# An attention, expert and MLP kernel: weight loads moved to the head of a step, three kinds of loads one or two steps later

## The chip, the cores and the metric

The program runs on one core of a Trainium2 chip. What counts is the device time of one execution, in microseconds (us). Beside the times there is one execution with a profile; its times are counted from the start of its span. Engines are called as the profile calls them: PE (TensorE), PEld (its weight loads), DVE (VectorE), ACT (ScalarE), POOL (GpSimd), SP (SyncE, which issues nearly all loads).

## What is computed

```python
def _attn_ref(q, k, v, f):                       # B, H, S, D = 2, 8, 576, 64
    scores = q @ k.T / sqrt(D)
    cum = np.cumsum(np.log(np.clip(f, 0.0001, 1.0)), axis=-1)
    scores = np.where(causal, -1e9, scores + cum[:, :, :, None] - cum[:, :, None, :])
    attn = exp(scores - max); attn = attn / (sum + 1e-9)
    return attn @ v
def _moe_ref(x, domain_probs, w1, w2):           # N, D, E, F = 1152, 512, 4, 1024
    p = domain_probs / (domain_probs.sum(-1) + 1e-9)
    for e in range(E): out += p[:, e:e+1] * (np.maximum(x @ w1[e], 0) @ w2[e])
def _moe2_ref(x, w_in, w_out):                   # d_ff = 2048
    h = x @ w_in
    return (h / (1 + exp(-1.702 * h))) @ w_out
```

The three follow each other: attention, four experts weighted per token, and an MLP. The code above is shortened from the reference.

## The kernel before

**Precision.** Operands are split into two parts, a rounded high one and a low rest (hi and lo), and a product takes three matmuls: hi by hi, lo by hi, hi by lo. Rounding a weight is an ACT instruction (`whi`, line 71), the low part a subtraction on DVE (`wlo`, line 249). Queries are rounded on POOL (`qhi`, line 68) and their low parts are made there (`qlo`, line 596); keys are rounded on ACT, their low parts made half on DVE and half on POOL (`ks`, line 578).

**Stages.** The tokens stand in four chunks. Chunk 0 (256 tokens) has its attention first. Then `attention()` works off the rest as a sequence of units: of chunk 1 three units for each pair of heads (384, 512 and 576 keys wide; 12 units, counted from 0 here), then of the second batch five units for each pair (20 units). A step of this generator emits scores for unit i (PE, line 652), the maximum on DVE (line 682, which also adds the gate row `cb` or, in the units of 576, `cbs`), the exponential of unit i - 1 on ACT (line 698) and its normalisation on POOL (line 708), the transposes of unit i - 2 (PE, line 726, copied out of PSUM by ACT, `ph`), and the product with the values of unit i - 3 (PE, line 756, tile `x`, rounded into `xh` and `xl`).

Into these steps the first layers (`emit_l1`, PE line 934) and second layers (`emit_l2`, line 1099) of the experts are mixed for chunks whose attention is done: the main loop walks the list `seq` of such visits and steps, and `pull()` takes as many attention steps as are due. So PE has the expert matmuls as filling for its waits in the attention. From about 200 us on only experts and the MLP are left; there some products are computed jointly for two chunks with sums and differences of weights (`emit_joint`, line 974, combined on DVE in `u` and `jc`), and the MLP's weights, which come as 64-bit numbers, are converted in steps of one instruction (`mlp_convert`, lines 418 to 433, tiles `cvt`, `wf`, `cvd`). How many of these steps are emitted behind a step of the main loop is counted in `cv_due`.

**What sets the order.** The engines take their instructions in the order that a scheduler gives them from the order of emission and its own model; only some parts are pinned by hand. SP's queue is in order too: a load that waits for its buffer holds up those behind it. Loads of weights go in pairs of 512 KB into four buffers (`wst`): when both halves of a pair are split, `rest()` puts the function `load_pair` on the list `pair_due`, and before the change it was called from the next `rest()` or from `split_next`.

**Loads of the attention.** In a step i, for the pair of heads whose first unit is i + 3, keys and queries are prepared (`prep_parts`, `prep_queries`), and the keys and queries (`kq`, `qr`) of the pair after it are loaded (`load_heads`) at the end of the step. For the pair that begins at i + 2 `load_cum` loads two `cb` tiles (128x512) and the `cbs` tile (128x576, in two halves). For the pair that begins at i the values (`vd`) are loaded.

Of the kernel before, what the change touches and what calls it, by code (L numbers as in the profile page):

```python
# [15 lines left out]
B, H, S, D = 2, 8, 576, 64  # L16
# [34 lines left out]
def attn_moe_mlp(ctx: ExitStack, tc: tile.TileContext, qk0, qk1, qk2, v0, vp, fg, dp, wa_moe, wb_moe, wa_mlp, wb_mlp, out):  # L51
# [36 lines left out]
    late = {}  # L88
# [506 lines left out]
            r, h, l = (t.rearrange("p (t g k) -> p t g k", g=2, k=128)[64 * g:64 * g + 64, :, g] for t in (raw, f(hi), lo))  # L595
            nc.gpsimd.tensor_sub(l, r, h)

    def load_cum(p, h0):

        cs, b, s0 = p  # L600
        st = pairs[p, h0]
        r = b * H + h0
        st["cb"] = [cb_p.tile([128, 512], F32, tag="cb", name="cb") for _ in range(2)]
        for g, cb in enumerate(st["cb"]):
            load(cb, cumd[r + g:r + g + 1, :512].to_broadcast([128, 512]))
        st["cbs"] = cbs_p.tile([128, S], F32, tag="cbs", name="cbs")
        for g in range(2):
            load(st["cbs"][64 * g:64 * g + 64], cumd[r + g:r + g + 1, :].to_broadcast([64, S]))
# [203 lines left out]
    def first_step(i):  # L812

        n = len(first_seq)
        p, h0 = passes[1], 0
        prep = [(7, lambda: prep_keys(p, h0, 0)), (7, lambda: prep_keys(p, h0, 1)), (9, lambda: prep_keys(p, h0, 2)),
                (9, lambda: prep_queries(p, h0, 1, (0,))), (9, lambda: prep_queries(p, h0, 1, (1,)))]
        for j in (0, 1) if i == 0 else (i + 1,):
            if j < n:
                emit_scores(*first_seq[j])  # L820
        if 3 <= i < n + 3:
            emit_pv(0, i - 3)
        if i >= 7 and x_used[0] < x_made[0] and x_used[0] < 3:
            emit_first(x_used[0])
            x_used[0] += 1
        if i < n:
            emit_max(*first_seq[i])
            emit_exp(*first_seq[i])
        if 1 <= i <= n:
            emit_norm(*first_seq[i - 1])  # L830
        if 2 <= i < n + 2:
            first_copy(i - 2)
        if 3 <= i < n + 3:
            emit_x2(0, i - 3)
        split_rest()
        for kind, p0 in (("a", 2), ("b", 6)):
            if 0 <= i - p0 < 4:
                split_w(kind, 0, i - p0)
                pass
        for j, fn in prep:  # L840
            if i == j:
                fn()
        if i < len(FILL):
            turn(FILL[i])
        if 1 <= i <= n:
            first_tr(i - 1)
        if i == 0:
            load_cum(p, h0)
        if i == 8:
            load_heads(passes[1], 2)  # L850
        if i == 9:
            load_values(p, h0)

    def attention():
# [9 lines left out]
        for i, (c, u) in enumerate(seq):  # L864
            if True:
                first_q.setdefault((pass_of[c], u[0][0], c), i)
        nxt = list(first)
        per_unit = dict(scores=emit_scores, max=emit_max, exp=emit_exp, norm=emit_norm, tr=emit_tr)
        by_last = dict(pv=emit_pv, x2=emit_x2)
        names = sorted(STAGES, key=lambda k: -STAGES[k])  # L870
        for i in range(len(seq) + L_X2 + 1):
# [8 lines left out]
                    prep_queries(*k)  # L880
            for k in [k for k in nxt if first[k] == i + 2]:
                load_cum(*k)
            for k in [k for k in nxt if first[k] == i and i]:
                load_values(*k)
            for k in names:
                j = i - STAGES[k]
                if k in per_unit:
# [9 lines left out]
            for k in new:  # L897
                n = nxt.index(k) + 1
                if n < len(nxt):
                    load_heads(*nxt[n])  # L900
            yield done


# [447 lines left out]
    cv_due = [0]  # L1351
    in_turn(emit_first, 3, True)
    for i, (kind, v_, b, c) in enumerate(seq):
# [22 lines left out]
            j_gen = emit_joint(v_, b, m, ts_rest, 0, 1) if kind == 7 else emit_joint(v_, b, m, ts, *visits[v_][1][:2])  # L1376
        n_steps = steps(kind, v_, b, c)
        for g in range(n_steps):
            if kind in (2, 6):
                split_until("b", v_, range(4))  # L1380
            elif kind not in (4, 5):
# [55 lines left out]
            if late:  # L1437

                if sums_at.get(u, 0) < 2:
# [4 lines left out]
                    else:  # L1444
                        rate = (0.75 if kind == 4 else 0) if v_ < v_all else 1.4 if v_ == v_all else 1.75
                    if kind == 3 and v_ in both_joint and c == EXP[0]:
                        cv_due[0] += g in (0, 2)
                    cv_due[0] += rate * (4 / n_steps) if rate != 11 / 4 else 3 * (g < 3)
                while cv_due[0] >= 1:
                    in_turn(next, cv_gen[0], None)  # L1450
# [66 lines left out]
```

## Time and profile before

| | |
|---|---|
| median of 3 runs | 692.91 us (691.76 to 693.12) |
| the profiled execution | 691.82 us, span 690.1 us |
| PE busy | 681.2 us, 99% of the span, 3937 matmuls |
| PEld, DVE, ACT, POOL busy | 600.0, 531.4, 354.3, 239.4 us |
| granted clock of PE | 0.999 of full speed |
| chain of work that ended last | PE 92%, DVE 4%, the rest 1% or less each |

The profiled execution's own time is 1.7 us more than its span. Matmuls are pipelined and their ends are modelled: a PE that is busy all the time may still lose some time between matmuls, and differences between starts tell more than the busy times.

### The profile page before, as it was taken

Reading aid. Unit: us, or ns where it says so; the run is one execution under the profiler, and the core shown is the slowest. Engines: PE = TensorE matmul, PEld = TensorE weight load, DVE = VectorE, ACT = ScalarE, POOL = GpSimd, SP = SyncE. Lnnn points to the kernel's source line nnn. Section 1 sums busy time; section 2 is a strip of 40 time slices with the busy share of each in tenths; the row PEclk is TensorE's granted clock in tenths of the full one; section 3 lists DMA queues with packets and bytes.
Section 4 is the critical chain, followed back from the end, with each engine's and each line's share of the span. In section 5 each row is a group of like instructions: output and inputs, shape, how many; then the busy total and the mean of one; then the engine's idle time right before and its main releaser. Section 6 shows DMA issues by size and latency. Waiting matters only on the chain.

```text
span 690.1 us, 11086 instructions
## 1 busy us (share of the span) xinstructions
PE 681.2 (99%) x3937; PEld 600.0 (87%) x3937; DVE 531.4 (77%) x1097; ACT 354.3 (51%) x821; POOL 239.4 (35%) x286
## 2 busy tenths in 40 slices
PE   8999999999999999999999999999999999999997
PEld 4797888888888998998889898898899998998986
DVE  6896777777789688676887878767799989998632
ACT  5778767667543645635246254362456454452420
POOL 6887576532233454543035324133003300120000
PEclk9999999999999999999999999999999999999999
DMA  8697726313542244144631422403332544441012
GB/s 251 229 301 249 258 93 238 99 61 93 168 138 61 51 134 129 48 128 157 196 107 47 144 86 82 146 33 107 123 107 77 153 138 136 154 153 61 1 47 91
DMA packets 41063, 87.59 MB, mean 127 GB/s; under 512 B 3720, under 2 KB 5776, under 8 KB 40752
## 3 DMA queue, kind: packets, MB, share of 16 engines
q1 hardware_dynamic: 40680, 84.75, 38.2%
q0 software_dynamic: 288, 2.10, 0.8%
q8 instruction: 31, 0.51, 0.3%
q14 instruction: 24, 0.20, 0.1%
q10 hardware_dynamic: 40, 0.04, 0.0%
HBM read 73.98 MB, written 12.88 MB: 126 GB/s over the span
## 4 chain that ended last, share of the span: by engine, by line
PE 92%; DVE 4%; POOL 1%; ACT 1%; DMA 1%; issue 1%; SPq 0%; POOLq 0%; DVEq 0%
PE m L1099 41%; PE m L974 23%; PE m L934 15%; PE s L652 4%; PE x L756 4%; PE t L726 3%; PE m L1255 1%; DMA dpraw<-in_dp_dram 1%; DVE acc L1143 0%; POOL ks L578 0%; DVE hl L1088 0%; DVE cvd L431 0%; DVE wlo L249 0%; PE m L951 0%; DVE wf L433 0%
## 5 line engine op out<-in xcount | busy, mean ns | idle before, releaser
L1099 PE MATMUL m<-whi,hh 128*128 128x512 f32 x392 | 109.6, 392 | 0.0
L1099 PE MATMUL m<-wlo,hh 128*128 128x512 f32 x392 | 108.0, 391 | 0.0
L1099 PE MATMUL m<-whi,hl 128*128 128x512 f32 x392 | 107.2, 390 | 0.0
L249 DVE TENSOR_TENSOR wlo<-wst,whi 128x512 fp32r<-128x512 f32 x132 | 100.3, 774 | 5.1 <-ACT whi L71 4.6
L985 POOL TENSOR_TENSOR hl<-jc,hh 128x320 fp32r<-128x320 f32 (+1 forms) x60 | 53.1, 888 | 141.1 <-ACT hh L71 141.1
L71 ACT ACTIVATE whi<-wst 128x512 fp32r<-128x512 f32 x136 | 80.7, 625 | 23.7 <-PE m L1099 13.5
L1099 PEld LDWEIGHTS m<-wlo,hh 128*128 128x128 f32 x392 | 73.4, 188 | 15.5
L1099 PEld LDWEIGHTS m<-whi,hl 128*128 128x128 f32 x392 | 73.5, 188 | 15.5
L1099 PEld LDWEIGHTS m<-whi,hh 128*128 128x128 f32 x392 | 71.9, 188 | 12.4
L270 POOL TENSOR_TENSOR sr<-wst 128x256 f32<-128x256 f32 x20 | 17.9, 893 | 156.2 <-DMA wst<-wm 58.0
L708 POOL TENSOR_SCALAR e<-e,sm 128x128 f32<-128x128 f32 (+4 forms) x72 | 46.7, 660 | 60.3 <-DVE sm L706 35.9
L983 ACT ACTIVATE jc<-jc 128x320 f32<-128x320 f32 (+1 forms) x60 | 27.1, 451 | 54.8 <-DVE jc L980 54.3
L1143 DVE SCALAR_TENSOR_TENSOR acc<-m,dpn,acc 128x512 f32<-128x512 f32 x63 | 46.5, 744 | 9.0 <-PE m L1099 8.9
L934 PE MATMUL m<-xh,whi 128*128 128x256 f32 (+2 forms) x256 | 51.7, 316 | 0.0
L934 PE MATMUL m<-xl,whi 128*128 128x256 f32 (+2 forms) x256 | 51.7, 316 | 0.0
L934 PE MATMUL m<-xh,wlo 128*128 128x256 f32 (+2 forms) x256 | 51.0, 313 | 0.0
L698 ACT ACTIVATE e<-e,mx 128x128 f32<-128x128 f32 (+4 forms) x72 | 41.7, 581 | 11.6 <-DVE mx L682 11.1
L934 PEld LDWEIGHTS m<-xh,whi 128*128 128x128 f32 x256 | 41.6, 189 | 1.4
L934 PEld LDWEIGHTS m<-xl,whi 128*128 128x128 f32 x256 | 41.5, 189 | 0.8
L1082 ACT ACTIVATE m<-m 128x384 f32<-128x384 f32 x48 | 23.0, 480 | 37.3 <-DVE m L980 35.6
L934 PEld LDWEIGHTS m<-xh,wlo 128*128 128x128 f32 x256 | 41.5, 189 | 0.7
L71 ACT ACTIVATE ph<-t 128x256 f32<-128x256 f32 (+4 forms) x81 | 28.9, 405 | 17.6 <-PE t L726 17.2
(173 smaller groups left out, 1502.5 us busy)
## 6 DMA issues: line engine op xcount, KB each, us to landing
wst<-in_wa_moe_dram SPq DMA_DIRECT2D x28, 512.0 KB, 3.8
wst<-in_wb_moe_dram SPq DMA_DIRECT2D x28, 512.0 KB, 4.5
mst<-in_wa_mlp_dram SPq DMA_DIRECT2D x16, 512.0 KB, 3.7
wm<-wf SPq DMA_DIRECT2D x32, 256.0 KB, 3.9
mst<-in_wb_mlp_dram SPq DMA_DIRECT2D x16, 512.0 KB, 4.1
wst<-wm SPq DMA_DIRECT2D x16, 512.0 KB, 3.9
cb<-cumd SPq DMA_DIRECT2D x16, 256.0 KB, 4.0
qr<-in_qk_dram SPq DMA_DIRECT2D x8, 384.0 KB, 5.1
```

The lines of the kernel that those rows point to most:

```text
L71: return nc.scalar.activation(out=out, in_=in_, func=AF.Copy)
L249: (nc.gpsimd if v_ == 0 and kind == 'a' and g < 4 else nc.vector).tensor_sub(lf, raw, f(hf))
L652: nc.tensor.matmul(pt[:, :z - a], lhsT=lr[i][0], rhs=lr[i][1], start=i == 0 and not (both and pt is not bank), stop=i == n - 1, skip_group ...
L698: nc.scalar.activation(out=e[:, off:off + w], in_=e[:, off:off + w], func=AF.Exp, scale=-1.0, bias=mx, accum_out=sm[:, 0, k:k + 1])
L708: nc.gpsimd.tensor_scalar(out=e[:, off:off + w], in0=e[:, off:off + w], scalar1=sm[:, 0, i:i + 1], scalar2=1.0, op0=ALU.mult, op1=ALU.mult)
L756: nc.tensor.matmul(pt[64 * g:64 * g + 64, o:n], lhsT=lhsT, rhs=rhs, start=i == 0, stop=i == nk - 1)
L934: nc.tensor.matmul(p[:, :n], lhsT=w[:, k, :], rhs=x[c][:, k, :], start=(j == 0 and k == 0), stop=(j == 2 and k == 3))
L974: nc.tensor.matmul(p[:, :WN], lhsT=w[a][:, k, :], rhs=x[z][:, k, :], start=start and j == 0 and k == 0, stop=stop and j == 2 and k == 1, s ...
L983: nc.scalar.activation(out=r, in_=r, func=AF.Relu)
L985: nc.gpsimd.tensor_sub(hl[:, g, :], r, f(hh[:, g, :]))
L1099: nc.tensor.matmul(p, lhsT=h_tile(v_, b, c, j, x, k), rhs=wb[v_, k][w].rearrange("p a c -> p (a c)"), start=i == 0 and k == 0, stop=i == 2 ...
L1143: nc.vector.scalar_tensor_tensor(out=a, in0=p, scalar=d, in1=a, op0=ALU.mult, op1=ALU.add)
```

## The change

Four things are changed; the work that is computed stays the same, and so does the number of instructions on each engine.

1. In the main loop, until the attention is done, a `load_pair` that is owed is called at the head of each step, ahead of the attention steps that are pulled there.
2. `load_heads` for the next pair goes on a list `owed` and is called one attention step later, behind `load_cum` and ahead of `load_values`.
3. `load_cum` loads only the two `cb` tiles; the `cbs` tile is loaded by the new `load_last`, called with `load_values`, two steps later. For the first pair it stays where it was.
4. In the first step of the joint halves of expert visits (`both_joint`, first chunk) one conversion step is emitted behind g = 0 and g = 2; in the first of these visits now behind g = 0 only.

```diff
-    def load_cum(p, h0):
+    def load_cum(p, h0, first=False):
...
         for g, cb in enumerate(st["cb"]):
             load(cb, cumd[r + g:r + g + 1, :512].to_broadcast([128, 512]))
+        if first:
+            load_last(p, h0)
+
+    def load_last(p, h0):
...
         st["cbs"] = cbs_p.tile([128, S], F32, tag="cbs", name="cbs")
         for g in range(2):
             load(st["cbs"][64 * g:64 * g + 64], cumd[r + g:r + g + 1, :].to_broadcast([64, S]))
...
             for k in [k for k in nxt if first[k] == i + 2]:
                 load_cum(*k)
+            for k in owed:
+                load_heads(*k)
+            owed.clear()
             for k in [k for k in nxt if first[k] == i and i]:
                 load_values(*k)
+                load_last(*k)
...
                 if n < len(nxt):
-                    load_heads(*nxt[n])
+                    owed.append(nxt[n])
...
         for g in range(n_steps):
+            if not late:
+                while pair_due:
+                    pair_due.pop()()
...
                     if kind == 3 and v_ in both_joint and c == EXP[0]:
-                        cv_due[0] += g in (0, 2)
+                        cv_due[0] += g in (0, 2)[:1 + (v_ > v_all + 1)]
```

**What it moves in the attention, on SP and POOL.** SP's queue before, from the keys of the fourth pair of chunk 1; the second `kq` with the `qr` of 512 and of 768 belongs to the first pair of the second batch, and the `cb x2` behind it is the one that stands at 52.30 us in the trace:

```order
L77 DMA kq<-in_qk_dram 128x576
L77 DMA qr<-in_qk_dram 128x768
L77 DMA cb<-cumd 128x512 x2
L77 DMA cbs<-cumd 64x576 x2
L77 DMA wst<-in_wa_moe_dram 128x2x512
L77 DMA vd<-in_vp_dram 128x640
L77 DMA kq<-in_qk_dram 128x576
L77 DMA qr<-in_qk_dram 128x512
L77 DMA qr<-in_qk_dram 128x768
L77 DMA cb<-cumd 128x512 x2
L77 DMA cbs<-cumd 64x576 x2
L77 DMA wst<-in_wa_moe_dram 128x2x512
```

The same stretch with the change; the `cb x2` that stands at 52.30 us before is here the second one:

```order
L77 DMA wst<-in_wa_moe_dram 128x2x512
L77 DMA cb<-cumd 128x512 x2
L77 DMA kq<-in_qk_dram 128x576
L77 DMA qr<-in_qk_dram 128x768
L77 DMA wst<-in_wa_moe_dram 128x2x512
L77 DMA vd<-in_vp_dram 128x640
L77 DMA cbs<-cumd 64x576 x2
L77 DMA cb<-cumd 128x512 x2
L77 DMA kq<-in_qk_dram 128x576
L77 DMA qr<-in_qk_dram 128x512
L77 DMA qr<-in_qk_dram 128x768
L77 DMA wst<-in_wa_moe_dram 128x2x512
```

The weight loads stand further ahead, `cbs` behind `vd`, and the keys and queries (`kq`, `qr` of 512 and 768) behind the `cb` loads that stood behind them.

POOL from one normalisation of a 576-wide unit (unit 2) to the next (unit 5), before:

```order
L708 TENSOR_SCALAR e<-e,sm 128x576
L68 TENSOR_SCALAR qhi<-qr 128x512
L596 TENSOR_TENSOR qlo_0_134<-qr,qhi 64x2x128 x2
L708 TENSOR_SCALAR e<-e,sm 128x384 x2
L676 MEMSET e 128x64
L708 TENSOR_SCALAR e<-e,sm 128x512 x2
L68 TENSOR_SCALAR qhi<-qr 128x768
L596 TENSOR_TENSOR qlo_1_133<-qr,qhi 64x3x128 x2
L578 TENSOR_TENSOR ks<-kq,ks 64x576
L708 TENSOR_SCALAR e<-e,sm 128x576
```

and with the change:

```order
L716 TENSOR_SCALAR e<-e,sm 128x576
L716 TENSOR_SCALAR e<-e,sm 128x384 x2
L684 MEMSET e 128x64
L716 TENSOR_SCALAR e<-e,sm 128x512 x2
L68 TENSOR_SCALAR qhi<-qr 128x768
L68 TENSOR_SCALAR qhi<-qr 128x512
L596 TENSOR_TENSOR qlo_1_133<-qr,qhi 64x3x128 x2
L578 TENSOR_TENSOR ks<-kq,ks 64x576
L596 TENSOR_TENSOR qlo_0_134<-qr,qhi 64x2x128 x2
L716 TENSOR_SCALAR e<-e,sm 128x576
```

The rounding of the 512-wide queries moves behind that of the 768-wide ones, their low parts behind the keys; the ten rows are the same ones.

**On PE.** From the last part of an `x` product to the transposes of units 4 (eight) and 5 (the four and one of a 576-wide e), before; `x12` are the eight and the four:

```order
L756 MATMUL x<-ph,vd 64x64 x2
L726 MATMUL t<-identr,e 128x128 x6
L652 MATMUL s<-ks,qhi 128x384
L655 MATMUL s<-tri,identr 128x128
L652 MATMUL s<-ks,qhi 128x384
L655 MATMUL s<-tri,identr 128x128
L652 MATMUL s<-ks,qlo_0_132 128x384 x2
L934 MATMUL m<-xh,wlo 128x256 x4
L934 MATMUL m<-xl,whi 128x256 x4
L726 MATMUL t<-identr,e 128x128 x12
L934 MATMUL m<-xh,whi 128x256 x2
L652 MATMUL s<-ks,qhi 128x512
```

With the change, the rows behind the eight transposes (which stand just ahead of the first row) up to the four:

```order
L946 MATMUL m<-xh,whi 128x256
L660 MATMUL s<-ks,qhi 128x512
L663 MATMUL s<-tri,identr 128x128
L660 MATMUL s<-ks,qlo_0_132 128x512
L946 MATMUL m<-xh,whi 128x256
L946 MATMUL m<-xh,wlo 128x256
L660 MATMUL s<-ks,qhi 128x512
L663 MATMUL s<-tri,identr 128x128
L660 MATMUL s<-ks,qlo_0_132 128x512
L946 MATMUL m<-xh,wlo 128x256 x3
L946 MATMUL m<-xl,whi 128x256
L734 MATMUL t<-identr,e 128x128 x4
```

The four transposes are parted from the eight by two groups of 512-wide scores and seven expert matmuls (`m`). Further up, seven expert matmuls more stand ahead of the `x` product, and seven more between the 384-wide scores and the eight transposes.

**On DVE, in the first of the joint halves.** The combinations `u` and `jc` and the conversions around them, before:

```order
L419 TENSOR_SCALAR cvt<-cvt 128x512
L1017 TENSOR_TENSOR u_4343<-m,u_4343 128x320
L422 TENSOR_SCALAR cvt<-cvt 128x512
L1020 TENSOR_TENSOR u_4344<-m,u_4343 128x320
L980 TENSOR_TENSOR jc<-m,u_4344 128x320
L980 TENSOR_TENSOR jc<-u_4344,m 128x320
L1045 SCALAR_TENSOR_TENSOR hl<-m,hh 128x320
L980 TENSOR_TENSOR jc<-m,u_4343 128x320
L425 SCALAR_TENSOR_TENSOR wf<-mst,cvt 128x512
```

and with the change:

```order
L419 TENSOR_SCALAR cvt<-cvt 128x512
L1029 TENSOR_TENSOR u_4343<-m,u_4343 128x320
L1032 TENSOR_TENSOR u_4344<-m,u_4343 128x320
L992 TENSOR_TENSOR jc<-m,u_4344 128x320
L992 TENSOR_TENSOR jc<-u_4344,m 128x320
L1057 SCALAR_TENSOR_TENSOR hl<-m,hh 128x320
L992 TENSOR_TENSOR jc<-m,u_4343 128x320
L422 TENSOR_SCALAR cvt<-cvt 128x512
L425 SCALAR_TENSOR_TENSOR wf<-mst,cvt 128x512
```

The conversion at line 422 moves from between the two `u` to behind the last `jc`, and those behind it move on by one.

## Rows read from the trace of the kernel before

**Rows 1.** Windows: stretch, its us, busy us (x instructions), PEclk, DMA share, GB/s.

```profile
60.00:70.00 10.00, 8.55 (x66) 6.97 (x65) 5.99 (x17) 8.07 (x22) 5.45 (x7) 1.00 0.89 329
...
340.00:350.00 10.00, 9.95 (x54) 8.69 (x53) 8.80 (x15) 3.72 (x9) 5.02 (x6) 1.00 0.32 82
...
570.00:580.00 10.00, 10.00 (x46) 8.29 (x45) 9.86 (x19) 5.37 (x11) 0.00 (x0) 1.00 0.46 131
```

**Rows 2.** Waits, PE, 30 to 200 us: total us, times, longest us.

```profile
PE t L726 <- POOL e L708: 1.4, 1, 1.4
```

**Rows 3.** Waits, PEld, 200 to 690 us.

```profile
PEld m L974 <- DVE jc L980: 0.3, 1, 0.3
```

**Rows 4.** Timeline of PE, 59 to 64 us: start, us, engine, line, operation [idle before].

```profile
59.20 0.64 PE L934 MATMUL m<-xl,whi 128*128 128x256 f32 x4
59.67 1.04 PE L726 MATMUL t<-identr,e 128*128 128x128 f32 x8
62.16 0.66 PE L726 MATMUL t<-identr,e 128*128 128x128 f32 x4 [1.45 <-POOL e L708]
62.57 0.48 PE L934 MATMUL m<-xh,whi 128*128 128x256 f32 x2
62.89 0.41 PE L652 MATMUL s<-ks,qhi 128*128 128x512 f32 x1
...
63.48 0.41 PE L934 MATMUL m<-xh,whi 128*128 128x256 f32 x2
```

**Rows 5.** Timeline of POOL, 50 to 62 us and at 87 us.

```profile
50.95 1.08 POOL L68 TENSOR_SCALAR qhi<-qr 128x512 fp32r<-128x512 f32 x1
52.12 1.53 POOL L596 TENSOR_TENSOR qlo<-qr,qhi 64x256 fp32r<-64x256 f32 x2
...
56.28 1.33 POOL L68 TENSOR_SCALAR qhi<-qr 128x768 fp32r<-128x768 f32 x1
57.69 2.09 POOL L596 TENSOR_TENSOR qlo<-qr,qhi 64x384 fp32r<-64x384 f32 x2
59.86 1.40 POOL L578 TENSOR_TENSOR ks<-kq,ks 64x576 fp32r<-64x576 f32 x1
61.36 0.74 POOL L708 TENSOR_SCALAR e<-e,sm 128x576 f32<-128x576 f32 x1
...
87.76 0.84 POOL L68 TENSOR_SCALAR qhi<-qr 128x768 fp32r<-128x768 f32 x1
```

**Rows 6.** Timeline of ACT, 40 to 75 us.

```profile
48.80 0.63 ACT L71 ACTIVATE whi<-wst 128x512 fp32r<-128x512 f32 x1 [3.10 <-DMA wst<-in_wa_moe_dram]
...
61.77 1.15 ACT L71 ACTIVATE whi<-wst 128x512 fp32r<-128x512 f32 x2 [3.23 <-DMA wst<-in_wa_moe_dram]
```

**Rows 7.** Timeline of SP's queue, 50 to 60 us.

```profile
52.30 1.00 SPq L77 DMA_DIRECT2D cb<-cumd  x2
...
57.87 0.54 SPq L77 DMA_DIRECT2D wst<-in_wa_moe_dram  x1
```

**Rows 8.** DMA issues: count, KB each, median us from issue to landing.

```profile
wst<-in_wa_moe_dram SPq DMA_DIRECT2D x28, 512.0 KB, 3.8
...
qr<-in_qk_dram SPq DMA_DIRECT2D x4, 256.0 KB, 4.1
```

**Rows 9.** Timeline of DVE, 341 to 344 us.

```profile
341.74 0.42 DVE L422 TENSOR_SCALAR cvt<-cvt 128x512 uint32<-128x512 uint32 x1
...
342.66 0.49 DVE L980 TENSOR_TENSOR jc<-m,u 128x320 f32<-128x320 f32 x1
```

**Rows 10.** Tile qr: ns minimum/median/maximum, first and last start; its landings.

```profile
L596 POOL TENSOR_TENSOR qlo<-qr,qhi x24: 727/1013/1416, 30.3 to 139.4; 64x384 fp32r<-64x384 f32 x16, 64x256 fp32r<-64x256 f32 x8
...
DMA to landing us min/median/max: 3.9/4.9/6.8
```

**Rows 11.** Tile ks, on POOL.

```profile
L578 POOL TENSOR_TENSOR ks<-kq,ks x8: 1400/1748/1885, 27.3 to 132.5; 64x576 fp32r<-64x576 f32 x8
```

**Rows 12.** Line 249, 36 to 70 us.

```profile
L249 DVE TENSOR_TENSOR wlo<-wst,whi x14: 675/695/1915, 35.4 to 69.4; 128x512 fp32r<-128x512 f32 x14
```

More of the change, by code (lines that the diff above doesn't have):

```diff
@@ L605, in load_cum @@
             load(cb, cumd[r + g:r + g + 1, :512].to_broadcast([128, 512]))
+        if first:
+            load_last(p, h0)
+    def load_last(p, h0):
+        cs, b, s0 = p
+        st = pairs[p, h0]
+        r = b * H + h0
         st["cbs"] = cbs_p.tile([128, S], F32, tag="cbs", name="cbs")
@@ L847, in first_step @@
         if i == 0:
-            load_cum(p, h0)
+            load_cum(p, h0, True)
         if i == 8:
@@ L866, in attention @@
                 first_q.setdefault((pass_of[c], u[0][0], c), i)
-        nxt = list(first)
+        nxt, owed = list(first), []
         per_unit = dict(scores=emit_scores, max=emit_max, exp=emit_exp, norm=emit_norm, tr=emit_tr)
```

## The prediction

> **What bounds the kernel now.** I read the views in this order: the table of windows, the waits of TensorE, its timeline where it waits, and then back along the engines that it waited for. The windows first [rows 1]: at a granted clock of 1.00, the upper of its two levels (2.4 GHz), TensorE is busy 10.00 of 10 us nearly everywhere; the two short windows shown, 60 to 70 us (8.55) and 340 to 350 us (9.95), are the only ones between 40 us and the last ten. There the time is TensorE's own work, which the change leaves as it is, plus what it waits. Its waits are few: 1.4 us on POOL's normalisation in the attention [rows 2] and 0.3 us on a DVE combination later [rows 3]. These two are all that a change of order can win there; what it can lose is new waits of the same kind.
>
> The timeline shows the first wait [rows 4]. Eight transposes start at 59.67. Four that do not wait for each other take 0.41 us (62.16 to 62.57), so eight take 0.8 to 0.9 and the next could start at 60.5; they start at 62.16. That is **1.6 us lost**, start to start (the 1.45 us in the row counts from a modelled end). They read the 576-wide e of unit 5, which POOL had normalised at 61.36 + 0.74 = 62.10 [rows 5]. POOL was late because it had worked without a gap since 50.95: on the 512-wide queries of a later pair (50.95 and 52.12), then, once unit 5's scores had freed the buffers, on the 768-wide queries (56.28, 57.69) and the keys (59.86). A second engine was late at the same place: ACT idled 3.23 us until 61.77 for a weight load [rows 6] that SP had issued only at 57.87 [rows 7]. Mending POOL's order alone would have gained little: the next weights for TensorE were rounded only from 61.77 on.
>
> **Weight loads at a step's head.** This changes no work, only SP's queue. The load issued at 57.87 now stands ahead of two cb loads that have to wait for a maximum, so ACT's 3.23 us go. With these weights there, the scheduler gives TensorE 14 matmuls of 256 columns ahead of the eight transposes (7 ahead of the x product, 7 behind the scores) that stood behind the wait before, and between the eight and the four 7 more and two groups of 512-wide scores. Four such matmuls take 0.47 us (59.20 to 59.67), 0.12 each; a score group takes 63.48 - 62.89 = 0.59 [rows 4]. TensorE therefore comes to the four transposes at 60.5 + 21 x 0.12 + 2 x 0.59 = **64.2 us**, with useful work up to then.
>
> The same move puts one weight load ahead of the third pair's keys, near 28 us. I cost that at nothing: the weight's buffer comes free within some 5 us, and the keys are wanted later than that plus a landing. If the cover is too short, TensorE waits for these scores before 58 us.
>
> **Keys and queries one step later.** POOL's work up to unit 5's normalisation is the same in sum, but the 512-wide queries now stand behind the 768-wide ones, and their load stands behind the two cb loads. Those go out at 52.30 and take 1.00 us [rows 7]; with the keys in between, the queries go out at about 53.8. Loads of queries of this size land 4.1 us after issue in the median [rows 8]: 57.9 us. From there POOL needs, with durations and gaps of its rows [rows 5], 1.2 (512-wide queries rounded) + 4.4 (57.69 to 62.10: 768-wide low parts, keys, normalisation) + 1.6 (512-wide low parts) = 7.2 us. The normalisation ends at **65.1 us**; TensorE, there at 64.2, waits 0.9 us instead of 1.6: **-0.7 us**.
>
> What else is near: the weight load behind these queries goes out at about 54.9 and lands at 58.7 by its median of 3.8 us [rows 8]. ACT takes it (0.6 us a weight, [rows 6]) ahead of the copies that free the PSUM buffers for the eight transposes, which TensorE now reaches at 59.67 + 14 x 0.12 = 61.4. That fits at the median. Were the load 2 us later, TensorE would wait 1 us there, but would then come 1 us later to the four transposes, where it waits anyway: the two do not add. Keys and queries of the pair after that are also issued some us later; POOL takes them at 87.76 [rows 5], so nothing waits.
>
> **Last gate rows two steps later.** Each step's cbs rows are first read two steps after the new place of their load, some 11 us, and no load of [rows 8, 10] takes longer than 6.8. Cost nothing.
>
> **One conversion step less.** In the first of the joint halves the chain of DVE operations has no gap; a conversion of 0.42 us at 341.74 stands between two combinations, and TensorE waits for the jc at 342.66 [rows 9]. Without it jc starts some 0.4 us earlier and the wait of 0.3 us [rows 3] goes: **-0.3 us**. Later conversions stand one step further back. DVE has 9.86 busy of 10 us at 570 [rows 1], so that could hurt, but the sum of its work is unchanged and TensorE shows no wait there now. I put it at 0.
>
> **Switches.** In the moved piece TensorE enters one more group of transposes, and the x product is broken once. Behind a group of transposes two matmuls take 62.89 - 62.57 = 0.32 us instead of 0.24 [rows 4], so a switch costs 0.1: two make **+0.2 us**.
>
> **The sum** is -0.7 - 0.3 + 0.2 = -0.8 us against the profiled execution (691.82 us; span 690.1): 691.0. That execution is 1.1 us below the median of the three runs, 692.91; on the median's scale I forecast **692.1 us**. About 0.2% (1.4 us) is what a measurement of this kernel can tell from no change, so I call this the same. The unknown is the queries' landing: 3.9 us after issue at best and 6.8 at worst [rows 10], which makes the wait 0.7 to 3.6 us.
>
> **Rivals.** *The whole wait goes.* The two cb loads wait for maxima on DVE, and DVE's subtractions stood behind ACT, which idled 3.10 us for a weight load at 48.80 [rows 6]; that load comes early now, too. If the cb loads leave 0.9 us sooner, all that follows is 0.9 us sooner and TensorE waits for nothing: -1.6 - 0.3 + 0.2 = -1.7, 691.2 us on the median's scale. Against it: DVE has other work ahead of those maxima, which stays. Chance 0.25. By the Trainium skill (DMA: Bandwidth & Descriptors, Anatomy of one DMA) a transfer takes about 2.0 us plus its bytes over 436 GB/s; an estimate by that page is 2.6 us for 256 KB, and the queries would then be early enough without that. No row here is so short, so the rows decide.
>
> *POOL slows down.* DVE's subtractions waited with ACT until 61.77 and now come earlier, beside POOL's low parts and keys. Such rows differ: keys on POOL take 1.40 us at the least and 1.885 at the most [rows 11], one low part 0.73 to 1.42 [rows 10], a weight subtraction on DVE 0.695 in the median and up to 1.915 [rows 12]. The piece in question had short values (1.40, and 2.09 for two). At the long ones it takes 0.5 + 0.7 us more, TensorE waits 2.1 us, and the sum is +0.5 - 0.3 + 0.2 = +0.4: 693.3 us, no change. Chance 0.10. By the Trainium skill (SBUF — State Buffer, Who interferes with whom) a DVE instruction with two SBUF inputs and a GpSimd instruction that reads SBUF shut each other out for a whole instruction. The rows agree in kind; it speaks against this change, which fills DVE's hole.
>
> *The queries come too late: slower.* They stand in SP's queue behind the cb loads and in POOL's queue ahead of the normalisation. If they land 6.8 us after issue, at 60.6, the normalisation ends at 67.8, TensorE waits 3.6 us, and the sum is +2.0 - 0.3 + 0.2 = +1.9 us: 694.8 us. It passes 0.2% from a landing of 6.3 us on. For it: several loads leave together here. Against it: the median of all query loads is 4.9 us [rows 10]. Chance 0.15.
>
> That the change doesn't do what it says is excluded: the new order shows each move.
>
> **Numbers.** The forecast has 0.50, with a range of its own from 691.6 to 692.8. The runs scatter by 1.4 us, so 0.05 goes from same to faster: same 0.50 + 0.10 - 0.05 = 0.55, faster by over 0.2% 0.25 + 0.05 = 0.30, slower 0.15. The range reaches from the first rival to the second, with half the scatter on either side, 690.5 to 694.0, and leaves out the third.
>
> **What would show it.** Right: ACT's idle times before weight loads at 48.8 and 61.8 us gone; POOL's normalisation for unit 5 ending near 65 us; a wait of 0.5 to 1.2 us of TensorE on it; none on jc; everything about 0.6 us earlier at 100 us, and 0.8 us from 345 us on. Wrong: no wait at all near 64 us, or one of over 2 us there; a new wait on a PSUM buffer or on keys between 30 and 130 us; a wait on DVE's conversions after 390 us.

## The result, and the profile after

The changed kernel takes **696.26 us** (median of 7 runs, 694.51 to 698.97) against 691.85 us before (7 runs beside it, 691.61 to 693.12): a ratio of 1.0062, 95% interval 1.0049 to 1.0074. It is slower by 0.6%, some 4.4 us; the forecast was 692.1 us, in a range of 690.5 to 694.0. The profiled execution has a span of 694.6 us, 4.5 more than before.

Two of the windows of [rows 1], now of the changed kernel (stretch, its us, busy us of PE, PEld, DVE, ACT and POOL with their instructions, PEclk, DMA share, GB/s):

```profile
60.00:70.00 10.00, 7.04 (x41) 6.44 (x40) 6.19 (x19) 7.28 (x20) 6.51 (x8) 0.83 0.43 128
340.00:350.00 10.00, 10.00 (x59) 9.17 (x59) 8.63 (x17) 3.61 (x9) 1.68 (x2) 1.00 0.56 160
```

The gap at 60 to 70 us, which the change was expected to halve, has doubled: 7.04 busy instead of 8.55. And the granted clock, 1.00 before, is 0.83 there. TensorE's waits, from 30 to 200 us and from 200 us on, are:

```profile
PE t L734 <- ACT ph L71: 3.1, 2, 3.0
PE s L660 <- POOL qlo L596: 0.4, 1, 0.4
...
PE m L986 <- DVE m L992: 0.4, 1, 0.4
```

POOL's normalisation is gone from this list [rows 2]. In its place stands ACT, with copies into ph, and at the end a sum on DVE that was not there. (L726 of before is L734 now, L756 is L764, L974 is L986, L980 is L992.) TensorE's timeline where it waits, and at the next pair's x product:

```profile
60.69 0.40 PE L946 MATMUL m<-xh,whi 128*128 128x256 f32 x2
64.05 1.81 PE L734 MATMUL t<-identr,e 128*128 128x128 f32 x8 [2.96 <-ACT ph L71]
...
68.54 0.60 PE L734 MATMUL t<-identr,e 128*128 128x128 f32 x4
...
85.89 0.75 PE L764 MATMUL x<-ph,vd 128*64 128x320 f32 x2
86.58 0.38 PE L946 MATMUL m<-xl,whi 128*128 128x256 f32 x1
86.89 2.15 PE L764 MATMUL x<-ph,vd 128*64 128x320 f32 x14
88.98 0.55 PE L734 MATMUL t<-identr,e 128*128 128x128 f32 x3
...
90.34 0.34 PE L764 MATMUL x<-ph,vd 128*64 128x64 f32 x4
90.61 0.55 PE L734 MATMUL t<-identr,e 128*128 128x128 f32 x3
```

The wait is in front of the eight transposes, not of the four behind them. The ACT and SP rows say why; ACT first:

```profile
57.37 0.18 ACT L706 ACTIVATION_READ_ACCUMULATOR e<-e,mx 128x1 f32 x1
62.57 0.63 ACT L71 ACTIVATE whi<-wst 128x512 fp32r<-128x512 f32 x1 [5.02 <-DMA wst<-in_wa_moe_dram]
63.10 0.42 ACT L71 ACTIVATE xh<-x 128x320 fp32r<-128x320 f32 x1
63.42 0.86 ACT L71 ACTIVATE ph<-t 128x384 f32<-128x384 f32 x2
```

SP's queue, with the load that ACT waited for:

```profile
51.87 1.33 SPq L77 DMA_DIRECT2D cb<-cumd  x2
53.26 0.42 SPq L77 DMA_DIRECT2D kq<-in_qk_dram  x1
53.73 0.90 SPq L77 DMA_DIRECT2D qr<-in_qk_dram  x2
54.73 0.38 SPq L77 DMA_DIRECT2D wst<-in_wa_moe_dram  x1
```

The two copies at 63.42 free the PSUM buffers of the eight transposes. Their transposes had run at 57.51, so they could have been copied from 58.4 on. But ACT works in order, and the rounding of one weight stands ahead of them. It waits for a load issued at 54.73 that lands at 62.5, 7.8 us later. Before, the rounding that waited [rows 6] stood behind these copies; ACT idled there as well, but held nothing that TensorE wanted at that time. Its row before that idle time:

```profile
57.67 0.88 ACT L71 ACTIVATE ph<-t 128x384 f32<-128x384 f32 x2
```

The windows of 2 us show what came on top (stretch, its us, busy us of PE with its matmuls, PEclk, DMA share, GB/s):

```profile
56.00:58.00 2.00, 2.00 (x23) 1.00 0.97 306
58.00:60.00 2.00, 2.00 (x18) 1.00 1.05 411
60.00:62.00 2.00, 1.09 (x10) 1.00 0.98 282
62.00:64.00 2.00, 0.00 (x0) 1.00 0.90 251
64.00:66.00 2.00, 1.95 (x10) 0.55 0.10 35
66.00:68.00 2.00, 2.00 (x9) 0.60 0.00 0
68.00:70.00 2.00, 2.00 (x15) 1.00 0.19 75
```

TensorE did nothing from 61.1 to 64.05, and when it starts again the granted clock is at 0.50, the lower of its two levels, until after 67 us. The 1.6 us idle of before had left it at 1.00 [rows 1, 4]. The last column but one matters, too: from 56 to 64 us the 16 DMA engines were all but full, after 0.76 from 54 to 56 us, when the late load went out.

### The profile page after: what moved, and what is told of

It is laid out like the page before. It is cut to its first block, busy times and chain, and to the rows that moved or that the text cites. A ratio compares the mean times of both kernels' runs of the same rounds, so it can differ in the third digit from the quotient of the medians.

```text
span 694.6 us, 11096 instructions
## 1 busy us (share of the span) xinstructions
PE 683.9 (98%) x3937; PEld 601.5 (87%) x3937; DVE 532.9 (77%) x1097; ACT 354.7 (51%) x821; POOL 237.6 (34%) x286
## 4 chain that ended last, share of the span: by engine, by line
PE 85%; DVE 7%; DMA 2%; ACT 2%; issue 2%; POOL 1%; SPq 0%; DVEq 0%; POOLq 0%; ACTq 0%
PE m L1111 39%; PE m L986 22%; PE m L946 12%; PE s L660 4%; PE x L764 4%; PE t L734 3%; DVE tr L330 1%; DVE wlo L249 1%; DMA wst<-in_wa_moe_dram 1%; DMA wst<-in_wb_moe_dram 1%; DVE hl L1438 1%; DVE tl L325 1%; DMA dpraw<-in_dp_dram 1%; DVE wf L425 1%; PE m L1267 0%
## 5 line engine op out<-in xcount | busy, mean ns | idle before, releaser
L249 DVE TENSOR_TENSOR wlo<-wst,whi 128x512 fp32r<-128x512 f32 x132 | 102.6, 790 | 8.1 <-ACT whi L71 7.6
```

The source lines that it names most:

```text
L249: (nc.gpsimd if v_ == 0 and kind == 'a' and g < 4 else nc.vector).tensor_sub(lf, raw, f(hf))
```

## Theories and experiments

**Theory 1**: the late load hurts by its place in SP's queue, behind keys and queries. **Theory 2**: the DMA engines are crowded, and the place in the queue changes little. **Theory 3**: the loss comes from the first part alone, which plans more matmuls on early weights. First each part of the change was undone by itself.

**Undo the second part** (keys and queries):

```diff
-                owed.append(nxt[n])
+                load_heads(*nxt[n])
```

> The change without its second part: keys and queries are again loaded one step earlier; weight loads at a step's head, the later gate rows and the conversion step stay. Theory 1 (the load's place): in the changed kernel the weight load of 54.73 us stands right behind kq and two qr, lands 7.8 us later at 62.49, ACT idles 5.0 us for it and holds the copies that the eight transposes need; with keys and queries out of its way that load lands by about 58, the 3.0 us wait of TensorE goes, so does the stretch at half clock behind it (64 to 67.7 us), and the kernel takes 692 to 693 us. Theory 2 (crowding: the 16 DMA engines are simply full, whatever the order): the load lands as late, a wait of 2.5 to 3 us stays, 695.5 to 696.5 us. Both leave the 0.4 us wait on DVE at 548 us.

Measured: 692.92 us, ratio 1.0012 (1.0003 to 1.0021). The time is that of theory 1, and the load landed in time (ACT waited 0.26 us for it, at 59.05). But another wait came, of 3.5 us, for POOL's normalisation at 66 us, which now stood behind the 768-wide low parts, and the granted clock fell behind it. (The profiled execution was the slowest of twelve, with a mean clock of 0.997; the three with a clock of 1.000 took 691.3 to 692.7 us.) So the load's place was mended, and yet TensorE waited: theory 1 alone does not decide.

**Undo the first part** (weight loads at the head):

```diff
-            if not late:
-                while pair_due:
-                    pair_due.pop()()
```

> The change without its first part: weight loads are issued at a step's end again; keys and queries later, gate rows later and the conversion step stay. Theory 1: the weight load stays behind the queries and moves later still by the half step, so ACT waits for it as in the changed kernel; a wait of 2 to 4 us near 62 us and 695.5 to 698 us. Theory 3 (the loss comes from the first part itself, which fills TensorE's order with matmuls that need weights early): the wait goes and the kernel takes 692 to 693 us.

Measured: 696.5 us, 1.0067 (1.0055 to 1.0079). Theory 3 falls. ACT idled 6.19 us for the same load, here with TensorE directly behind the weight:

```profile
63.84 1.22 PE L946 MATMUL m<-xh,whi 128*128 128x256 f32 x4 [4.50 <-ACT whi L71]
```

**Undo the third part** (last gate rows):

```diff
-        if first:
-            load_last(p, h0)
-    def load_last(p, h0):
...
-                load_last(*k)
```

> The change without its third part: the last gate rows are loaded with the first ones again, two steps earlier, so they stand in front of the keys, the queries and the weight load. Theory 1: the two cbs loads are in front of the late weight load, which is issued some 1 us later or more; the wait is as long or longer, 695.5 to 698 us. If instead the third part is the culprit (cbs in flight together with the weight load steals its bandwidth), the wait shrinks to about 1.5 us, the half-clock stretch goes, and 692.5 to 694 us come out.

Measured: 692.65 us, 1.0008 (0.9999 to 1.0017), no difference from before. The time and the short waits (0.8 us at most) are near those of the second reading, but its cause is not shown: the load was far later than in the changed kernel, and the wait was short all the same. ACT and SP of this kernel:

```profile
58.49 0.87 ACT L71 ACTIVATE ph<-t 128x384 f32<-128x384 f32 x2
...
66.49 1.15 ACT L71 ACTIVATE whi<-wst 128x512 fp32r<-128x512 f32 x2 [4.64 <-DMA wst<-in_wa_moe_dram]
```

```profile
56.53 1.95 SPq L77 DMA_DIRECT2D cbs<-cumd  x2
...
60.16 0.38 SPq L77 DMA_DIRECT2D wst<-in_wa_moe_dram  x1
```

ACT idles 4.64 us for the weight, but *behind* the two copies. The gate rows (cbs) wait on DVE and hold SP's queue until 56.5, and the copies stand first. In the changed kernel nothing holds the queue there, the load goes out 5.4 us earlier, and the rounding stands first. I take it that the scheduler's model expects the landing in time there; no run shows the model itself. That is **theory 4**: not the load's lateness but the order on ACT, made for a load that lands sooner than it does. It can be tested with everything else held.

**The held order.** For the kernels below the order of the changed kernel on all five engines was written into a table, and each instruction was tied to the one ahead of it:

```python
    held = {i.name: i for i in nc.cur_bb.bb.instructions}
    for order in HELD:
        names = ["I-%d" % n for n in order]
        for one, two in zip(names, names[1:]):
            tc.add_manual_dep(held[two], one, ...)
```

So a single instruction can be moved with no other order changed. No run has this table without a move. In its place stand the rows of the next kernel: from 10 to 60 us its matmuls keep the changed kernel's order and start 0.4 us later throughout.

**The rounding four places later on ACT** (and its subtraction on DVE behind xl and two maxima):

```diff
-whi<-wst
 xh<-x
 ph<-t x2
 hh<-m
+whi<-wst
```

> The changed kernel with its order held on every engine by a table, but for one weight: its rounding on ACT stands behind xh and the two copies of 384 columns (four places later), its subtraction on DVE behind xl and two maxima. The load itself stays as late. Theory 4 (the late load hurts because its rounding stands ahead of the copies that free the PSUM buffers of the eight transposes, on an engine that works in order): the eight transposes start at about 61 us instead of 64.05, TensorE then comes to the four transposes of unit 5 near 64 us and waits until POOL has normalised (65.7 us), 1.5 to 2 us; the half clock goes, as no wait is over 3 us; 693 to 694.3 us. Rival (the weight itself is what TensorE needs): the wait only moves behind the transposes, 695.5 to 696.5 us.

Measured: 694.85 us, 1.0043 (1.0028 to 1.0058), less won than expected. The interval overlaps that of the changed kernel, so the rows have to carry it, and by them theory 4 holds: the eight transposes start at 61.31 without a wait. The wait is now where the prediction had it, on the normalisation, and 2.0 us long. In the profiled execution the clock fell behind this idle time, where the expectation had it stay up; of the six executions the three with a mean clock of 0.998 took 695.1 to 696.8 us, the three with 1.000 took 693.7 to 694.6.

```profile
64.06 0.28 PE L946 MATMUL m<-xl,whi 128*128 128x256 f32 x1
66.37 0.79 PE L734 MATMUL t<-identr,e 128*128 128x128 f32 x4 [2.02 <-POOL e L716]
```

```profile
64.00:66.00 2.00, 0.34 (x3) 1.00 0.13 47
66.00:68.00 2.00, 1.63 (x8) 0.69 0.01 5
68.00:70.00 2.00, 2.00 (x7) 0.50 0.68 161
```

**In addition unit 5's normalisation first on POOL:**

```diff
+e<-e,sm 128x576
 qhi<-qr 128x512
 qlo<-qr,qhi x2
 ks<-kq,ks
 qlo<-qr,qhi x2
-e<-e,sm 128x576
```

> As the kernel with ACT's and DVE's later turn, and on POOL the normalisation of unit 5 stands ahead of the 512-wide queries, the low parts and the keys instead of behind them. Theory 4 with the prediction's step on POOL: neither wait is left between 58 and 68 us, or one under 0.5 us for the weight's rounding at 62.6 us; 691.5 to 693 us. What remains over the kernel before is then the broken x product at 85 us (some 1 us) and the wait on DVE at 548 us (0.5 us). If the queries are needed sooner than I think, a wait of TensorE for them appears behind 75 us.

Measured: 692.8 us, 1.0013 (1.0004 to 1.0021). Both waits are gone with two moves, but two shorter ones of the same kind are there, for copies into ph behind a rounding that waits for its load: 0.7 us at 68 and 2.2 us at 85 us. The profiled execution took 697.96 us; the granted clock was at 0.50 behind the second wait, and also near 12 us. A second run stands below.

**The load ahead of keys and queries, ACT's order as in the changed kernel:**

```diff
 cb<-cumd x2
+wst<-in_wa_moe_dram
 kq<-in_qk_dram
 qr<-in_qk_dram x2
-wst<-in_wa_moe_dram
```

> The changed kernel with its order held, but for SP: the late weight load stands ahead of kq and the two qr instead of behind them. Theory 1 (place in the queue): issued at about 53.3 us, it lands by 58.5 us, ACT's idle 5.0 us and the wait at 61 us go; the queries land some 1.5 us later, POOL ends unit 5's normalisation near 67 us and TensorE, there at 64, waits 2 to 3 us for that instead; 693.5 to 695.5 us. Theory 2 (crowded engines): the load lands at 60.5 us or later all the same and a wait of 1.5 us or more for the copies stays in front of the other.

Measured: 697.93 us, 1.0081 (1.0069 to 1.0093), a miss: slower still. The wait for the copies did go, as theory 1 has it (the load landed 5.6 us after issue), but the queries paid with their landing and POOL with them: TensorE waits 3.6 us for the normalisation, again with a fall of the clock.

```profile
PE t L734 <- POOL e L716: 3.6, 1, 3.6
```

So the 3.0 us wait was exchanged for this one. Why the kernel is slower still is not shown: its profile is 1.6 us behind the changed kernel's at 58 us already, before the move can have acted, with two waits for DVE's maxima (0.5 at 35 and 0.6 us at 50) among it, and 1.7 at the end. Of these six loads, whichever stood behind the others was late; theory 2 has its share.

**24 useless matmuls in the wait:**

```diff
+        for k in range(FILL_IN if len(l1_calls) == 8 else 0):
+            nc.tensor.matmul(p[:, :n], lhsT=whi[:, k % 4, :], rhs=xh[c][:, k % 4, :], start=k == 0, stop=k == FILL_IN - 1)
```

> The changed kernel with its order held, and 24 matmuls of 256 columns more (2.9 us) right where TensorE waits at 60.8 us: they write a PSUM tile that the group behind them starts anew, so they change no result and only keep TensorE busy. If the wait drops the clock and the lower clock costs what I read (1.5 us between 64 and 67.7 us), the transposes start at 64 us as before, the granted clock stays at 1.00 and the kernel takes 694.5 to 695.3 us, faster with more work. If the slow matmuls of 64 to 67.7 us have another cause, nothing is gained: 696 to 697 us.

Measured: 695.47 us, 1.0050 (1.0038 to 1.0062), 0.2 us above the expected range. More work and, by the medians, 0.8 us less time than the changed kernel; the two intervals overlap, so the rows have to carry it:

```profile
61.10 3.04 PE L948 MATMUL m<-xh,whi 128*128 128x256 f32 x24
...
64.66 1.06 PE L734 MATMUL t<-identr,e 128*128 128x128 f32 x8 [0.28 <-ACT ph L71]
...
67.71 0.60 PE L734 MATMUL t<-identr,e 128*128 128x128 f32 x4
```

The same matmuls from the eight transposes to the four take 67.71 - 64.66 = 3.05 us here, at a granted clock of 1.00, and 68.54 - 64.05 = 4.49 in the changed kernel. The lower clock costs **1.4 us**.

**Undo the fourth part** (the conversion step), and **the fourth part alone** on the kernel before (the same line, the other way round):

```diff
-                        cv_due[0] += g in (0, 2)[:1 + (v_ > v_all + 1)]
+                        cv_due[0] += g in (0, 2)
```

> The change without its fourth part: the conversion step is there again. The attention is that of the changed kernel, wait and half clock included. Theory 1 puts 0.4 to 0.6 us of the loss on this part (TensorE waits 0.4 us at 548 us for a DVE sum, where four POOL additions ran beside DVE's conversions, which took up to twice as long) and a gain of 0.15 us at 342 us: 695.8 to 696.1 us, with the wait at 548 gone. The rival, that this wait is an accident of timing and not of the conversion's place, gives 696.3 us and the wait still there.

> The kernel before with the fourth part alone: one conversion step less in the first joint half. Theory 1: 0.15 to 0.3 us are won near 342 us, and 0.4 to 0.6 us lost near 545 us, where POOL's additions now meet DVE's conversions and TensorE waits for a DVE sum; 692.1 to 692.4 us. Rival (the wait at 548 us belongs to the attention's shift): no such wait, 691.6 to 691.8 us.

Measured: 695.8 us, 1.0058 (1.0045 to 1.0071), and 692.31 us, 1.0005 (0.9996 to 1.0014). In time neither can be told from no effect. In the profiles both are as expected: without the part no matmul waits from 300 us on, and with it the wait on DVE's sum is there (0.3 us), without any change to the attention. POOL and DVE of the kernel with the part alone:

```profile
538.04 1.28 POOL L270 TENSOR_TENSOR sr<-wst 128x256 f32<-128x256 f32 x1 [11.17 <-DVE cvd L431]
...
541.17 1.07 POOL L273 TENSOR_TENSOR sr<-wst,sr 128x256 f32<-128x256 f32 x1
```

```profile
538.65 0.96 DVE L419 TENSOR_SCALAR cvt<-cvt 128x512 f32<-128x512 f32 x1
...
544.23 0.42 DVE L419 TENSOR_SCALAR cvt<-cvt 128x512 f32<-128x512 f32 x1
...
545.15 0.57 DVE L980 TENSOR_TENSOR m<-m,u 128x384 f32<-128x384 f32 x1
```

The same conversion takes 0.96 us beside POOL's four additions and 0.42 after them. One step later in the conversions, POOL's additions are later, too, and meet the conversions ahead of the sum that TensorE wants. Before, the first of them was:

```profile
534.82 0.97 POOL L270 TENSOR_TENSOR sr<-wst 128x256 f32<-128x256 f32 x1 [8.97 <-DMA wst<-wm]
```

The Trainium skill (SBUF — State Buffer, Who interferes with whom) says that tensor_scalar on DVE can take the port pair that it shares with GpSimd, and that the later of the two then stands still; the rows agree in kind. That moving POOL's additions alone ends the wait was not tried.

**The second and the third part alone** on the kernel before:

```diff
+                owed.append(nxt[n])
-                    load_heads(*nxt[n])
```

> The kernel before with the second part alone: keys and queries one step later. The two cbs loads, which wait for maxima, still stand ahead of them and of the weight load. Theory 5: the weight goes out near 60 us, late for the plan too, so its rounding is planned behind the copies; waits of 1 to 1.5 us in all between 60 and 68 us at full clock, 691.5 to 693 us. Rival (the second part alone does the harm): a wait of 3 us or more and 695 us.

> The kernel before with the third part alone: the last gate rows two steps later. Keys and queries still stand ahead of cb, so SP is not held by their maxima before the weight load. Theory 5 (it takes the second and third part together to send six loads out within 3 us and to make the plan count on the weight too early): the order stays close to that of before, with the weight load out near 54 us instead of 57.87; no wait over 2 us, full clock, 691 to 692.5 us. Rival (the third part alone does the harm): a wait of 3 us at 60 to 64 us and 695 us or more.

Measured: keys and queries later, 691.5 us, 0.9998 (0.9989 to 1.0007); gate rows later, 693.77 us, 1.0019 (1.0010 to 1.0028), above its expected range. The second part is harmless alone, the third costs 0.2% alone, at full clock with no wait over 1.2 us. Every kernel that has both and the scheduler's own order has the large loss, with the first part or without it, and none with only one of them has it: **theory 5** (it takes the second and third part together) holds for the large loss. With only one of them something in the queue (the gate rows that wait for DVE, or a weight ahead of the keys) keeps cb, kq, two qr and wst from going out within 3 us. Many loads at once are not enough, though: with the second part alone cbs, kq, qr and wst, six loads again, left within 2.8 us, and the weight landed after 6.1 us, but its rounding stood behind the copies, and TensorE waited for nothing between 54 and 70 us.

**The x product in one piece,** everything else as in the kernel with the two moves, which ran again beside it:

```diff
+m<-xl,whi
 x<-ph,vd x2
-m<-xl,whi
 x<-ph,vd x14
+x<-ph,vd x4
...
-x<-ph,vd x4
```

> As the changed kernel with the later turn on ACT and DVE and unit 5's normalisation first on POOL, and in addition the x product at 86 us in one piece: on TensorE the one matmul of the weights goes in front of it, its last four matmuls follow the sixteen others, and on ACT the two copies of 64 columns that these four read come right behind the four copies of 512. If the broken product is worth what its rows say (3.2 us instead of 2.2), 691.5 to 692.2 us against 692.8 us in pieces, which leaves of the change's loss only the 0.4 to 0.6 us on DVE at 548 us. If the pieces cost no more than 0.1 us a switch, as the prediction had it, 692.6 to 693 us.

> The kernel with the later turn and unit 5's normalisation first once more, beside the one with the x product in one piece, on the same chip: 692.3 to 693.2 us, with the product in three pieces of 3.2 us in all, and no wait over 1 us between 58 and 90 us (the first profile of this kernel was of an execution 5 us above its median).

Measured: 692.29 us, 1.0005 (0.9996 to 1.0014), against 693.62 us, 1.0021 (1.0011 to 1.0031): 1.3 us. Both are above their expected ranges, the first by 0.1 and the second by 0.4 us. (The kernel with the two moves was at 692.8 us in its first run; the two runs differ by as much as their intervals allow.) In one piece:

```profile
83.17 2.46 PE L764 MATMUL x<-ph,vd 128*64 128x320 f32 x20
85.55 0.55 PE L734 MATMUL t<-identr,e 128*128 128x128 f32 x3
```

That is 2.4 us from start to start. In the changed kernel the first two pieces take 88.98 - 85.89 = 3.1 us, with one other matmul in them, and the third 90.61 - 90.34 = 0.3: 3.2 without that matmul. Before it was one piece of 2.2:

```profile
83.37 2.28 PE L756 MATMUL x<-ph,vd 128*64 128x320 f32 x20
85.58 0.88 PE L726 MATMUL t<-identr,e 128*128 128x128 f32 x6
```

Not all of the 1.3 us is the product. The kernel with the two moves waits 1.2 us just ahead of it, more than its expectation allowed, and the kernel with the product in one piece 0.8; that is 0.3 us of the difference between starts, and the product is 1.0, as its rows say. The waits of the former from 30 us on, for copies into ph:

```profile
PE t L734 <- ACT ph L71: 1.8, 2, 1.2
```

The wait is of the same kind as the large one: copies behind a rounding that waits for its load, 2.52 us here and 2.70 with the product in one piece. So the two moves mended one place, and the next late weight does the same on a smaller scale.

**The kernel before, with two instructions moved:**

```diff
 SP:   cb<-cumd x2
+SP:   wst<-in_wa_moe_dram
 SP:   cbs<-cumd x2
-SP:   wst<-in_wa_moe_dram
+POOL: e<-e,sm 128x576
 POOL: qhi<-qr 128x768
 POOL: qlo<-qr,qhi x2
 POOL: ks<-kq,ks
-POOL: e<-e,sm 128x576
```

> The kernel before with its order held on every engine by a table, but for two places: on SP the weight load that went out at 57.87 us stands ahead of the two cbs loads that wait for a maximum, and on POOL the normalisation of unit 5 stands ahead of the 768-wide low parts and the keys. Nothing else of the change. Theory 4: the load goes out near 54.5 us into queues with little in them and lands by 59, the normalisation ends near 59 us, so TensorE's 1.6 us at 60.4 us go and nothing takes their place: 690.0 to 690.7 us, below both kernels. Rival: the weight's rounding or the later low parts become the next wait, 691.5 to 692.5 us.

On POOL the normalisation stands ahead of the rounding of the 768-wide queries, too, which the expectation doesn't name.

Measured: **690.86 us**, 0.9979 (0.9970 to 0.9988), faster than both kernels, 0.2 us above the expected range. The two waits left from 30 us on are of 0.4 us each. The twelve transposes follow each other, the normalisation done at 58.6 us:

```profile
59.10 0.64 PE L934 MATMUL m<-xl,whi 128*128 128x256 f32 x4
59.58 1.48 PE L726 MATMUL t<-identr,e 128*128 128x128 f32 x12
60.81 0.48 PE L934 MATMUL m<-xh,whi 128*128 128x256 f32 x2
```

```profile
57.88 0.74 POOL L708 TENSOR_SCALAR e<-e,sm 128x576 f32<-128x576 f32 x1 [2.23 <-DVE sm L706]
```

The 1.6 us of before could be had: 1.7 us between starts in the two profiles, 1.1 by the medians. The two moves were not tried apart.

## Why the prediction was wrong

**What held.** The bound, the place of the first wait and its cause on POOL: the kernel before with two instructions moved wins just that wait. The queries' issue ("about 53.8", measured 53.73), their landing ("57.9", 58.8: POOL's idle time ended there) and the end of the normalisation ("65.1", 64.99 + 0.75 = 65.7) were near.

**The step that failed** is the landing of one weight: "the weight load behind these queries goes out at about 54.9 and lands at 58.7 by its median of 3.8 us. ... That fits at the median." It went out at 54.73 and landed at 62.5, after 7.8 us instead of 3.8. The median was that of 28 loads all over the kernel. This one left as the last of six within 3 us (51.87 to 54.73), and from 56 us on the engines were all but full. With only the two cb loads ahead of it the same load took 4.7 us (third part alone), 5.3 (without the second part) and 5.6 (moved ahead of the keys). The loads behind it shared the engines, too: vd and the two cbs left from 57.64 on, before it had landed. How much each took is not shown. The Trainium skill (DMA: Bandwidth & Descriptors, Issuing engines are not separate DMA queues) says that transfers started by different engines interleave on the same 16 DMA engines; these loads all left SP's queue, so no run here shows it for two issuers. The trace of before had the price for this stretch; weight loads issued from 40 to 75 us, five of them, have in the view of the tile wst:

```profile
DMA to landing us min/median/max: 3.8/6.2/7.1
```

The two with 6.5 and 7.1 us are those that went out at 60.40 and 60.94, right behind kq and two qr. The prediction's "no load of [rows 8, 10] takes longer than 6.8" rests on medians and on the queries; a weight took longer there. The step's consequence was stated rightly (ACT takes the weight ahead of the copies that free the PSUM buffers), but a lateness of 2 us was tried, not of 4, and the text then let the two waits cover each other. At 3.1 us lost start to start there was nothing left to cover: **+1.5 us** where the sum had -0.7. The -0.7 would not have come without the late weight either: with its rounding moved back, TensorE waited 2.0 us for the normalisation and not 0.9, as the queries landed 0.9 us later than by their median and the 512-wide low parts took 1.86 us on POOL instead of 1.53.

**A term that was missing:** the clock. Behind an idle time of 3 us TensorE was at its lower level for the next 3 us and more, **+1.4 us**; with the gap filled it was not. No row of before showed that, because its longest idle time in the middle of the kernel was 1.6 us, at full clock.

**A term that was mis-sized:** "the x product is broken once", at 0.1 us a switch. In the changed kernel the product of a later pair stands in three pieces, and these cost **1.0 us** by rows (and 1.0 between starts in the kernel where that alone was mended). The price was read from a switch behind transposes, not from one inside an x product.

**The conversion step** was put at -0.3 us with "TensorE shows no wait there now. I put it at 0" for the rest. The wait on jc fell only from 0.3 to 0.2 us, and a wait of 0.4 us, **0.5 us** between starts, came at 548 us. It is near the sign of being wrong that the prediction named, a wait on DVE's conversions: TensorE waits for a sum that the conversions held up. Its sum was that of DVE's work; that POOL's additions move with the conversions was not followed.

Together these are 1.5 + 1.4 + 1.0 + 0.5 - 0.1 = 4.3 us. The spans differ by 4.5, but in the profile of the changed kernel TensorE is 0.6 us early from 10 to 50 us, so the loss behind that is 5.0. Of the 0.7 us left, 0.3 between starts are a wait for copies at 85.13 us, of the same kind as the large one; the rest stays open. The early start is not the change's: the kernel in which only the rounding was moved has the same order up to there and is 0.4 us later.

**The rivals.** The slower one had the right sign, the right queue and the wrong load: queries late by their landing, where the weight behind them was. What it warned of came true when the weight was put ahead (3.6 us wait on the normalisation). In the first rival, the 2.6 us for 256 KB was far from these queries, which landed 5.0 us after issue; the Trainium skill (DMA: Bandwidth & Descriptors, Anatomy of one DMA) has that formula as a fit for transfers that GpSimd issues, and these left SP's queue. The rival of the shared port has little to show where it was put (POOL's low parts and keys took 2.08, 1.40 and 1.86 us against 2.09, 1.40 and 1.53); what looks like it came 480 us later, on DVE.

## What to carry to other kernels

A load's landing is priced by what is in flight with it, not by its median over the kernel: count the bytes that go out together, above all when a change takes away something that held the queue. On an engine that works in order, ask of each instruction that waits for a load what stands behind it; here a weight that landed at 66.5 us behind free work cost TensorE 0.8 us, and one that landed at 62.5 in front of two small copies cost 3.1. And an idle stretch of TensorE can have a second price, which comes after it: 1.4 us here.

## What the runs showed of the hardware

- After 3.0 us without a matmul the granted clock was at 0.50 for over 3 us, and in two other kernels after 2.0 and 2.2 us as well; after 1.6 us it had stayed at 1.00. Work that nobody reads, put into the gap, kept it at 1.00.
- Weight loads of 512 KB landed 3.8 us after issue in the median of 28 and 7.8 us where one left as the last of six within 3 us, at a DMA share of 0.76 first and then 0.90 to 1.05 until it had landed. In another kernel the last of six within 2.8 us, of fewer bytes, took 6.1 us.
- Twenty matmuls into the two halves of an x tile take 2.2 to 2.4 us in one piece, 0.27 to 0.31 for a pair of 320 columns. With another matmul behind it such a pair took 0.69 us, and that matmul 0.31 instead of 0.12: some 0.6 us for one break, where a switch behind transposes cost 0.1 [rows 4].
- A conversion on DVE took 0.96 us beside POOL's additions and 0.42 us without them.
